# Attention outputs through VectorE's block transposes and transfers instead of TensorE transposes, in an fp32 adaLN transformer block

## The chip, the cores and the metric

The kernel runs on one core of one Trainium2 chip. Its time is the device time of that core in microseconds, as the median of three runs. The core has a matrix engine (TensorE, PE in the profile; its weight loads are listed apart as PEld), a vector engine (VectorE, DVE), a scalar engine (ScalarE, ACT), GpSimd (POOL) and SyncE (SP), which here only issues transfers. All five run their own instruction streams and wait for each other through semaphores. [...]

## What is computed

One block of a transformer with adaptive layer norm, in fp32: 2048 tokens (S), width 576 (D), 32 heads of width 18, a feed-forward width of 4608.

```python
mod = (_silu(c) @ w_mod).reshape(c.shape[0], 6, 1, -1)
h = _layernorm(x, axis=-1) * (1 + ca) + sa
# A: qkv = h @ wqkv, split in heads
scores = jnp.einsum("bhqd,bhkd->bhqk", q, k) * (Dh ** -0.5)
p = _softmax(scores, axis=-1)
o = jnp.einsum("bhqk,bhkd->bhqd", p, v)
x = x + ga * (o @ wo)
h = _layernorm(x, axis=-1) * (1 + cb) + sb
x = x + gb * (_silu(h @ w1) @ w2)
```

The weights are scaled up by factors of 8 and 64, so the scores are large and the maximum of each row of scores must be taken off before the exponential.

## The kernel before

**Arithmetic.** Matrix products run in a fast fp32 format with fewer bits. Each operand is therefore split into a high part, which that format holds exactly, and a low part, and three products are summed (high by high, high by low, low by high).

**Tiling.** The queries are cut in four blocks of 512 (`NQB`), the heads in eight groups of four (`NQUAD`). A *quad* is four heads of one block, so there are 32 quads. Each quad has 32 *slots*, and each slot has two halves, `j` = 0 and 1.

**Two passes over the scores.** A slot of the first pass (`slot_a`, with the matmul on line 678) computes *row scores*: a tile with 128 queries as rows and 512 keys as columns. VectorE takes the maximum over the columns from PSUM (line 680). This pass serves only the maxima. A slot of the second pass (`slot_b`, line 735) computes the scores again with keys as rows and 512 queries as columns, and ScalarE takes the exponential (line 737). The maxima enter the second product as two extra rows of the query tile `qt` (rows 54 and 55 of each half, high and low part), against rows of ones in the key tile `kt`; so the product comes out with the maximum already subtracted. The second pass runs `LEAD` slots behind the first. `LEAD` is 38, so six slots lie between the last maximum of a quad and the first use of the maxima.

**The maxima's way.** After slot 31 of a quad, `max_a` (lines 693 to 700) reduces over the key blocks, negates and splits in two parts. Four half slots later (`MB`), `max_b` transposes them on TensorE into a bank of the row scores' pool (tile `pst`, line 704), VectorE copies them out (`mt`, line 709), and `max_rows` (line 714) places them in `qt` by four transfers.

**The outputs' way.** `pv` (line 772) multiplies the exponentials by V. Each head uses 32 rows of one PSUM bank: 18 output features, one row for the sum of the exponentials, and padding; the 512 queries are the columns. ScalarE copies the bank to `ov` (line 776). Then `out_b` (lines 781 to 801) transposes it on TensorE to queries as rows (`pso`, four transposes into one bank of the row scores' pool), VectorE takes the reciprocals of the sums and multiplies (lines 788 and 794), and the result goes to the block's tile `ot`. `out_b` asks the plan for 440 ns of TensorE; it may be put off by up to 12 half slots. After the eighth quad of a block, `post` queues the block's projection and MLP as *filler*: first `o_T` (lines 859 to 872), which transposes `ot` back to features as rows on TensorE (tile `psT`, 20 transposes a block) and splits it in a high part (ScalarE) and a low part (VectorE); then the projection by `wo` (`proj`, 28 steps for each of four groups of 128 queries), the second layer norm (`ln_a`, `ln_c`), its transposes (`h_T`), and the feed-forward products (`mlp1`, `mlp2`). The last part of a block's second product, 32 items, is held back in a list `left` and put in between the next block's projections: eight ahead of each of the first three, six and two later.

**What sets the order.** TensorE's order is written out: a planner (`Plan`, and the loop at the end of the body) keeps estimates of VectorE's and ScalarE's work and of when PSUM banks come free, and picks among a score step, a PV step and a filler item. The filler is spread over the slots by a pace. The start (`start_tasks`) is ordered by a small list scheduler of its own, and contains the first `LEAD` slots of the first pass. The orders of the other engines and of SP's transfers come from the framework, by priority and by readiness in its own estimate of time. PSUM has two or three banks for row scores, two or three for the second pass, one for PV and one to three for the filler.

**Buffers.** K lies in 14 tiles `kt` (`NKB`), filled eight slots ahead (`KLD`); `qt` has three buffers, `ov` one, and the tile `ot` one. The second layer norm writes its result over `ot`.

Of the kernel before, what the change touches and what calls it, by code (L numbers as in the profile page):

```python
# [39 lines left out]
LEAD = 38  # L40
# [15 lines left out]
MB = 4  # L56
# [3 lines left out]
LP0 = 1000  # L60
LP = 8000
# [271 lines left out]
def tile_adaln_block(ctx: ExitStack, tc: tile.TileContext, x, wqkv, wo, w1, w2, c, wfirst, wcol, out):  # L333
# [348 lines left out]
    def slot_a(s, j):  # L682
        if j == 0:
            slot_load(s)
        t = quads[s // 32]
        slot_mm(s, j)()
        plan.op("V", plan.t + TL - TS, TMAX, plan.take("a"))
        if j == 1 and s % 32 == 31:
            now = 2 * s + 1
            later.append((now, 0, 0, lambda: max_a(t), None))  # L690
            later.append((now + MB, 3, 110, lambda: max_b(t), lambda: t.get("ms_at")))

    def max_a(t):
        negm = at1.tile([P, 4, NST], F32, name="negm", bufs=2)
        nc.vector.tensor_reduce(negm, t["mx"], axis=AX.X, op=ALU.max, negate=True)
        ms = at1.tile([P, 2, 4, NST], F32R, name="ms", bufs=2)
        nc.vector.tensor_copy(ms[:, 0], negm)
        nc.vector.tensor_sub(ms[:, 1], negm, f(ms[:, 0]))
        t["ms"] = ms
        chain([("V", 230), ("V", 180), ("V", 180)], plan.t, None, lambda at: t.update(ms_at=at + TR))  # L700

    def max_t(t):
        ps = aux([P, 512], "pst")
        nc.tensor.transpose(ps[:32, :P], f(t["ms"]).rearrange("p c h s -> p (c h s)"), ident)
        return ps

    def max_copy(t, ps):
        t["mt"] = at1.tile([32, P], F32R, name="mt", bufs=2)
        nc.vector.tensor_copy(t["mt"], ps[:32, :P])

    def max_rows(t):
        for i in range(4):
            r0 = 64 * (i % 2) + 54 + i // 2
            nc.sync.dma_start(f(t["q"][r0:r0 + 1].rearrange("o h (a s) -> o (h a) s", s=P)), f(t["mt"][8 * i:8 * i + 8, :]))

    def max_b(t):
        max_copy(t, max_t(t))
        plan.op("V", plan.t, 270, plan.take("a"))
        max_rows(t)
# [45 lines left out]
    def pv(i, t, k0, n):  # L765
# [8 lines left out]
        if k0 + n == NKT:  # L774
# [4 lines left out]
            later.append((state["now"] + 2, 12, 440, lambda: out_b(i, ov), lambda: t["ov"]))  # L779

    def out_b(i, ov):
        b, qd = divmod(i, NQUAD)
        ps = aux([P, NST, P], "pso")
        for s4 in range(NST):
            nc.tensor.transpose(ps[:, s4, :], ov[:, s4 * P:(s4 + 1) * P], ident)  # L785
        rec = att.tile([P, NST, 4], F32, name="rec", bufs=2)
        psr = ps.rearrange("p s (h c) -> p s h c", h=4)
        nc.vector.reciprocal(rec, psr[:, :, :, DH])
        if qd == 0:
            if b:  # L790
                fill.until("h_T")
            o[b] = att.tile([P, NST, 640], F32, tag="o", name="ot", bufs=1)
        for s4 in range(NST):
            nc.vector.tensor_mul(o[b][:, s4, 72 * qd:72 * qd + 72].rearrange("p (h c) -> p h c", h=4), psr[:, s4, :, :DH],
                                 rec[:, s4, :, None].to_broadcast([P, 4, DH]))
        rel = plan.take("a")
        chain([("V", 260)] + [("V", 225)] * 4, plan.t + 100, None, rel)
        del quads[i]
        if qd == NQUAD - 1:
            nc.gpsimd.tensor_copy(o[b][:, :, D:640], o[b][:, :, 512:D])  # L800
            post(b)
# [48 lines left out]
    def post(b):  # L850
# [4 lines left out]
        ob = o[b]  # L855
# [3 lines left out]
        def o_T(kt):  # L859
# [3 lines left out]
            ps = bank("psT", psF)  # L863
            for j in range(NST):
                nc.tensor.transpose(ps[:, j * P:(j + 1) * P], ob[:, j, kt * P:(kt + 1) * P], ident)
            hi = c["th"][:, kt, :]
            chain([("A", 600), ("V", 690)], plan.t, None, plan.take("f"))
            nc.scalar.activation(hi, ps, AF.Copy)
            if kt < 4:
                nc.vector.tensor_sub(c["tl"][:, kt, :], ps, f(hi))  # L870
            else:
                nc.vector.tensor_sub(hi[64:], ps[64:], f(hi)[64:])
# [30 lines left out]
        def ln_c(j):  # L903
            mv, rs = c["ln", j]
            ln_apply(c["x1"][j], ob[:, j, :], mv[:, 0, :], rs, nc.vector)

        def h_T(kt):
# [5 lines left out]
            for j in range(NST):  # L913
                nc.tensor.transpose(ps[:, j * P:(j + 1) * P], ob[:, j, kt * P:(kt + 1) * P], ident)
# [9 lines left out]
        for kt in range(KT):  # L924
            fl.add(440, lambda kt=kt: o_T(kt), need=bank_need, mode="full")
        if b == 0:
            fl.add(LP0)
        for j in range(NST):
            rest(8 if j < 3 else 0)
            for part in range(len(GP)):  # L930
                fl.add(MMH * len(GP[part]), lambda j=j, part=part: proj(j, part), need={0: pair_need, len(GP) // 2: half_need}.get(part))
# [130 lines left out]
    def start_tasks(st):  # L1062
# [296 lines left out]
        for s in range(LEAD):  # L1359
# [9 lines left out]
            if s == 31:  # L1369
                t0 = add("V", 0.59, lambda: max_a(quads[0]), maxes, 8)  # L1370
                kt_ = tok("a")
                t1 = add("P", 0.11, lambda: d.update(pst=max_t(quads[0])), [t0], 8, take=kt_, mode="full")
                t2 = add("V", 0.27, lambda: max_copy(quads[0], d["pst"]), [t1], 8, free=kt_)
                dma(40e3, lambda: max_rows(quads[0]), [t2], 8)
# [183 lines left out]
```

## Time and profile before

| | |
|---|---|
| median of 3 runs | 2488.08 us (2486.09 to 2492.14) |
| span of the profiled execution | 2488.8 us |
| mean granted TensorE clock in it | 0.992 |
| TensorE busy | 2407.3 us, 97% |
| VectorE busy | 1772.8 us, 71% |
| ScalarE busy | 1501.9 us, 60% |
| GpSimd busy | 611.3 us, 25% |

The profiled execution's own time is given only as its span; it is 0.7 us above the median of the runs. In a row of a group, the text before the first bar is line, engine, operation, output and inputs with shapes, and the count. After the bar come the busy time in us and the mean of one in ns, and after the second bar the idle time of the engine just before these instructions, with what ended it. Timeline rows begin with the start in us and the length in us; "x4" means that four like instructions were merged; brackets give idle time before them. Matmuls overlap, and the profile models their ends. "DMA_DIRECT2D" on SPq is the issuing of a transfer. The first 160 us are the start (layer norm, the first Q, K and V products), then come four attention blocks of about 440 to 540 us, of which the last three have the previous block's MLP beside them; from 2212 us the last block's projection and MLP run alone.

### The profile page before, as it was taken

Reading aid. Unit: us, or ns where it says so; the run is one execution under the profiler, and the core shown is the slowest. Engines: PE = TensorE matmul, PEld = TensorE weight load, DVE = VectorE, ACT = ScalarE, POOL = GpSimd, SP = SyncE. Lnnn points to the kernel's source line nnn. Section 1 sums busy time; section 2 is a strip of 40 time slices with the busy share of each in tenths; the row PEclk is TensorE's granted clock in tenths of the full one; section 3 lists DMA queues with packets and bytes.
Section 4 is the critical chain, followed back from the end, with each engine's and each line's share of the span. In section 5 each row is a group of like instructions: output and inputs, shape, how many; then the busy total and the mean of one; then the engine's idle time right before and its main releaser. Section 6 shows DMA issues by size and latency. Waiting matters only on the chain.

```text
span 2488.8 us, 51319 instructions
## 1 busy us (share of the span) xinstructions
PE 2407.3 (97%) x20192; PEld 1581.2 (64%) x20192; DVE 1772.8 (71%) x3156; ACT 1501.9 (60%) x2736; POOL 611.3 (25%) x753
## 2 busy tenths in 40 slices
PE   6999999998989999999999999999999999999999
PEld 5774444434556666666666666666666666678988
DVE  7878878887777777777877777778777777334333
ACT  4237777776666666666666666666666666742121
POOL 4201011121566566652211111111211111110000
PEclk9999999999899999999999999999999999999999
DMA  7843334342455555553543433432633343226463
GB/s 242 261 135 114 109 110 122 105 150 91 135 182 185 168 180 180 198 168 123 173 145 127 146 124 126 134 132 95 209 127 122 126 162 116 103 101 242 171 221 119
DMA packets 159394, 372.02 MB, mean 149 GB/s; under 512 B 17754, under 2 KB 55034, under 8 KB 159154
## 3 DMA queue, kind: packets, MB, share of 16 engines
q1 hardware_dynamic: 154562, 366.45, 43.8%
q8 instruction: 160, 2.62, 0.4%
q10 hardware_dynamic: 4592, 2.29, 0.3%
q14 instruction: 80, 0.66, 0.1%
HBM read 282.35 MB, written 85.80 MB: 148 GB/s over the span
## 4 chain that ended last, share of the span: by engine, by line
PE 87%; DVE 7%; ACT 2%; issue 1%; POOL 1%; DMA 1%; SPq 0%; ACTq 0%; DVEq 0%; POOLq 0%
PE ps L470 26%; PE psv L772 19%; PE psa L678 14%; PE ps L464 10%; PE psb L735 8%; PE psqk L551 4%; DVE mx L680 3%; PE psv L470 2%; PE psp L470 2%; PE psqk L1211 1%; PE pso L785 1%; PE psv L1211 1%; DVE etmp L987 1%; PE psp L464 1%; ACT pt L737 1%
## 5 line engine op out<-in xcount | busy, mean ns | idle before, releaser
L680 DVE TENSOR_REDUCE mx<-psa 128x1 f32<-128x512 f32 x2048 | 1345.5, 686 | 379.1 <-PE psb L735 278.3
L737 ACT ACTIVATE pt<-psb 128x512 f32<-128x512 f32 x2048 | 1162.2, 598 | 549.5 <-PE psb L735 413.2
L735 PE MATMUL psb<-qt,kt 56*128 56x512 f32 x2048 | 789.8, 429 | 6.7 <-DMA qt<-mt 5.0
L678 PE MATMUL psa<-kt,qt 54*128 54x512 f32 x2048 | 768.0, 425 | 24.7 <-DVE mx L680 20.8
L678 PEld LDWEIGHTS psa<-kt,qt 54*128 54x128 f32 x2048 | 344.1, 185 | 415.2 <-DVE mx L680 275.4
L772 PE MATMUL psv<-pt,vt 128*32 128x512 f32 x4096 | 535.0, 607 | 0.5 <-PE psa L678 0.5
L470 PE MATMUL ps<-w2t,g 64*128 64x288 f32 x4992 | 417.9, 294 | 0.2 <-ACT etmp L980 0.2
L470 PEld LDWEIGHTS ps<-w2t,g 64*128 64x128 f32 x4992 | 387.0, 186 | 36.1 <-issue 12.2
L470 PE MATMUL ps<-hh,w1t 64*128 64x512 f32 x2160 | 385.2, 395 | 0.9 <-POOL hh L405 0.8
L735 PEld LDWEIGHTS psb<-qt,kt 56*128 56x128 f32 x2048 | 348.9, 185 | 39.8 <-ACT pt L737 20.0
L470 PEld LDWEIGHTS ps<-hh,w1t 64*128 64x128 f32 x2160 | 220.7, 186 | 58.2 <-issue 10.6
L990 POOL TENSOR_TENSOR g<-etmp,g 128x512 fp32r<-128x512 f32 x108 | 138.4, 1298 | 405.4 <-ACT g L989 361.7
L895 POOL TENSOR_TENSOR x<-x,gt 128x288 f32<-128x288 f32 x116 | 92.7, 800 | 488.5 <-ACT gt L894 478.5
L772 PEld LDWEIGHTS psv<-pt,vt 128*32 128x32 f32 x4096 | 93.0, 108 | 178.8 <-issue 171.3
L470 PE MATMUL ps<-hl,w1t 64*128 64x512 f32 x864 | 186.5, 394 | 1.0 <-POOL hl L403 1.0
L891 DVE TENSOR_TENSOR x<-ps,x 128x288 f32<-128x288 f32 x184 | 83.9, 456 | 122.3 <-PE ps L464 71.0
L464 PE MATMUL ps<-w2t,g 128*128 128x288 f32 x960 | 130.6, 295 | 1.7 <-ACT g L989 0.9
L464 PEld LDWEIGHTS ps<-w2t,g 128*128 128x128 f32 x960 | 128.6, 188 | 3.3 <-ACT g L989 1.2
L986 ACT ACTIVATE eq<-ps 128x512 f32<-128x512 f32 x36 | 21.6, 599 | 146.3 <-PE ps L464 146.3
L464 PE MATMUL ps<-hh,w1t 128*128 128x512 f32 x360 | 106.9, 390 | 0.5 <-DVE hh L405 0.5
L470 PEld LDWEIGHTS ps<-hl,w1t 64*128 64x128 f32 x864 | 93.5, 186 | 18.0 <-POOL hl L403 2.5
L987 DVE SCALAR_TENSOR_TENSOR etmp<-etmp 128x512 f32<-128x512 f32 x108 | 78.1, 761 | 21.4 <-ACT etmp L986 21.4
(142 smaller groups left out, 2033.4 us busy)
## 6 DMA issues: line engine op xcount, KB each, us to landing
w1t<-w1s SPq DMA_DIRECT2D x108, 640.0 KB
w2t<-w2s SPq DMA_DIRECT2D x108, 576.0 KB
kt<-kscr SPq DMA_DIRECT2D x512, 108.0 KB
w1s<-w1t SPq DMA_DIRECT2D x36, 640.0 KB
w2s<-w2t SPq DMA_DIRECT2D x36, 576.0 KB
vt<-vscr SPq DMA_DIRECT2D x32, 608.0 KB
qt<-qscr SPq DMA_DIRECT2D x128, 108.0 KB
raw<-in_w SPq DMA_DIRECT2D x72, 160.0 KB
```

What stands on the lines that cost most here:

```text
L464: mm(self.ps[late], lhsT=lhsT, rhs=rhs, start=(i == 0), stop=(i == self.n - 1))
L470: done = mm(self.ps[g], lhsT=lhsT[rows], rhs=rhs[rows], start=(s == 0), stop=(s == 2 * self.n - 1))
L551: mm(qk_ps[0], lhsT=w[b][:, kt, :], rhs=(hTl if a else hTh)[:, kt, n * 512:(n + 1) * 512], start=(i == 0), stop=(i == 13))
L678: mm(ps, lhsT=t["q"][64 * j:64 * j + 54, hp, stt * P:(stt + 1) * P], rhs=t["k", kc, hp][64 * j:64 * j + 54, :], start=True, stop=True)
L680: return lambda: nc.vector.tensor_reduce(t["mx"][:, 2 * j + hp, stt, kc:kc + 1], ps, axis=AX.X, op=ALU.max)
L735: mm(ps, lhsT=t["k", kt // 4, hp][64 * e:64 * e + 56, kt % 4 * P:(kt % 4 + 1) * P], rhs=t["q"][64 * e:64 * e + 56, hp, :], start=True, sto ...
L737: nc.scalar.activation(t["P"][kt, hp][:, e, :], ps, AF.Exp, scale=SCALE)
L772: mm(t["ps"][32 * h:32 * h + 32, :], lhsT=t["v"][:, c0:c0 + 32], rhs=t["P"][kt, h // 2][:, h % 2, :], start=(kt == 0), stop=(kt == NKT - 1 ...
L891: nc.vector.tensor_add(c["x1"][j][:, hs], ps, c["x1"][j][:, hs])
L895: nc.gpsimd.tensor_add(c["x1"][j][:, hs], c["x1"][j][:, hs], t)
L987: nc.vector.scalar_tensor_tensor(t, t, 1.0, u, op0=ALU.add, op1=ALU.mult)
L990: (nc.vector if last else nc.gpsimd).tensor_tensor(g[:, 1, :], t, f(g[:, 0, :]), op=ALU.subtract)
```

## The change

- `LEAD` goes from 38 to 40.
- Maxima: `max_a` arranges the two parts so that one VectorE transpose of 32x32 blocks (128x32) gives rows of 32 queries. `max_rows` writes the result to DRAM (`mscr`) in one transfer and reads it back into `qt` by two, in runs of 32 values. The TensorE transpose, its bank, the copy, `max_b` and `MB` go. The transfers are issued right after `max_a`.
- Outputs: `out_b` transposes `ov` by 32x32 blocks on VectorE into a scratch part of the block's tile `ou`. There each head's 32 rows are 32 queries, and the columns are 16 blocks of 32. VectorE takes 16 reciprocals per row; GpSimd multiplies (VectorE for the last quad of a block); VectorE transposes back into `ov`. Transfers from SBUF to SBUF then place each head's 18 rows at the head's features in `ou`, features as rows. A head that crosses a multiple of 128 takes two transfers, and rows of the last, partial group of features are placed twice: 40 transfers a block. `out_b` asks for no TensorE time and runs two half slots after the last PV step.
- `o_T` has no transposes: ScalarE copies the high part from `ou`, and GpSimd subtracts for the low part (in the last block VectorE for even groups). It costs the filler nothing. The first projection of a block waits in the plan for `o["at", b]`, five us after the modelled end of `out_b`'s chain.
- The second layer norm gets a tile of its own (`ob`), which takes turns with `ou` in one buffer.
- The held-back items go 16 ahead of the first projection (`RA`), none between (`RB`), and the rest as before behind the fourth.

```diff
-LEAD = 38
+LEAD = 40
-MB = 4
+RA, RB = 16, 0
...
-            later.append((now, 0, 0, lambda: max_a(t), None))
-            later.append((now + MB, 3, 110, lambda: max_b(t), lambda: t.get("ms_at")))
+            later.append((now, 0, 0, lambda: (max_a(t), max_rows(t)), None))
...
-        nc.vector.tensor_copy(ms[:, 0], negm)
-        nc.vector.tensor_sub(ms[:, 1], negm, f(ms[:, 0]))
+        nc.vector.tensor_copy(ms[:, :, 0], neg)
+        nc.vector.tensor_sub(ms[:, :, 1], neg, f(ms[:, :, 0]))
+        t["mt"] = at1.tile([P, 32], F32, name="mt", bufs=2)
+        nc.vector.transpose(t["mt"], f(ms).rearrange("p j c h -> p (j c h)"))
...
     def max_rows(t):
-        for i in range(4):
-            r0 = 64 * (i % 2) + 54 + i // 2
-            nc.sync.dma_start(f(t["q"][r0:r0 + 1].rearrange("o h (a s) -> o (h a) s", s=P)), f(t["mt"][8 * i:8 * i + 8, :]))
+        scr = dram.tile([P, 32], F32, name="mscr", bufs=2)
+        nc.sync.dma_start(scr, t["mt"])
+        for j in range(2):
+            src = scr.rearrange("(g j r) t -> j r g t", g=4, j=2)[j]
+            dst = t["q"][64 * j + 54:64 * j + 56].rearrange("c h (a g t) -> c (h a) g t", g=4, t=32)
+            nc.sync.dma_start(f(dst), src)
...
-            later.append((state["now"] + 2, 12, 440, lambda: out_b(i, ov), lambda: t["ov"]))
+            later.append((state["now"] + 2, 0, 0, lambda: out_b(i, ov), None))
...
-        ps = aux([P, NST, P], "pso")
-        for s4 in range(NST):
-            nc.tensor.transpose(ps[:, s4, :], ov[:, s4 * P:(s4 + 1) * P], ident)
...
+        tt = ou[:, 4, :]
+        nc.vector.transpose(tt, ov)
+        blocks = tt.rearrange("p (b c) -> p b c", c=32)
+        rec = att.tile([P, 16], F32, name="rec", bufs=2)
+        nc.vector.reciprocal(rec, blocks[:, :, DH])
+        eng = nc.vector if qd == NQUAD - 1 else nc.gpsimd
+        eng.tensor_tensor(blocks[:, :, :DH], blocks[:, :, :DH], rec[:, :, None].to_broadcast([P, 16, DH]), op=ALU.mult)
+        nc.vector.transpose(ov, tt)
...
+                for r in (r0, r0 + 64) if kt == 4 else (r0,):
+                    nc.sync.dma_start(ou[r:r + n, kt, :], ov[p0:p0 + n, :])
...
-            ps = bank("psT", psF)
-            for j in range(NST):
-                nc.tensor.transpose(ps[:, j * P:(j + 1) * P], ob[:, j, kt * P:(kt + 1) * P], ident)
-            hi = c["th"][:, kt, :]
-            nc.scalar.activation(hi, ps, AF.Copy)
+            hi, src = c["th"][:, kt, :], o[b][:, kt, :]
+            nc.scalar.activation(hi, src, AF.Copy)
+            eng = nc.vector if last and kt % 2 == 0 else nc.gpsimd
             if kt < 4:
-                nc.vector.tensor_sub(c["tl"][:, kt, :], ps, f(hi))
+                eng.tensor_tensor(c["tl"][:, kt, :], src, f(hi), op=ALU.subtract)
...
-            fl.add(440, lambda kt=kt: o_T(kt), need=bank_need, mode="full")
+            fl.add(0, lambda kt=kt: o_T(kt))
+        rest(RA)
...
-            rest(8 if j < 3 else 0)
+            rest(RB if j else 0)
...
-                t1 = add("P", 0.11, lambda: d.update(pst=max_t(quads[0])), [t0], 8, take=kt_, mode="full")
-                t2 = add("V", 0.27, lambda: max_copy(quads[0], d["pst"]), [t1], 8, free=kt_)
-                dma(40e3, lambda: max_rows(quads[0]), [t2], 8)
+                dma(80e3, lambda: max_rows(quads[0]), [t0], 8)
```

56 lines of the change are left out of this document (24 added, 32 removed).

## The prediction

> **What bounds the kernel now.** I read the page's busy times first, then the chain of work that ended last, then busy times by stretch.
>
> ```profile
> span 2488.8 us, 51319 instructions
> PE 2407.3 (97%) x20192; PEld 1581.2 (64%) x20192; DVE 1772.8 (71%) x3156; ACT 1501.9 (60%) x2736; POOL 611.3 (25%) x753
> PE 87%; DVE 7%; ACT 2%; issue 1%; POOL 1%; DMA 1%; SPq 0%; ACTq 0%; DVEq 0%; POOLq 0%
> ```
>
> ```profile
> 170.00:600.00 430.00, 416.46 (x2482) 171.88 (x2475) 344.13 (x601) 311.65 (x594) 60.45 (x61) 0.99 0.36 118
> 670.00:1140.00 470.00, 459.75 (x4308) 304.16 (x4305) 358.18 (x593) 315.43 (x571) 286.54 (x397) 1.00 0.54 178
> 1225.00:1680.00 455.00, 452.74 (x4303) 303.12 (x4297) 346.63 (x583) 312.48 (x566) 68.68 (x66) 1.00 0.40 135
> ```
>
> The rows give PE, PEld, DVE, ACT and POOL busy time per stretch, then granted clock and DMA share. TensorE is the bound: 99.5% busy in the third row (the third quarter of the attention, with the second block's MLP beside it), 97% in the first, and 87% of the chain is its own work. So PE time that is taken away shortens the run one for one, unless what replaces it makes PE wait. VectorE is second, 80% busy in the first row.
>
> **What leaves PE.** Three kinds of transposes go: the attention outputs (`pso`, 4 a quad, 32 quads), the maxima (`pst`, 1 a quad), and the normalised outputs before the projection (`psT` at line 865, 20 a block, 4 blocks). PE instructions overlap, so I price a piece by the distance from its start to the start of the next work. The first two rows below are a `pso` and its successor, the next two a `pst`, the rest the `psT` of the first block.
>
> ```profile
> 219.91 0.66 PE L785 MATMUL pso<-ident,ov 128*128 128x128 f32 x4
> 220.50 1.07 PE L772 MATMUL psv<-pt,vt 128*32 128x512 f32 x8
> 1401.74 0.28 PE L704 MATMUL pst<-ident,ms 128*32 128x128 f32 x1
> 1401.96 0.73 PE L470 MATMUL ps<-hh,w1t 64*128 64x512 f32 x4
> 598.86 1.47 PE L865 MATMUL psT<-ident,ot 128*128 128x128 f32 x12
> 600.26 0.49 PE L678 MATMUL psa<-kt,qt 54*128 54x512 f32 x1
> 600.92 0.66 PE L865 MATMUL psT<-ident,ot 128*128 128x128 f32 x4 [0.17 <-DVE tl L870]
> 601.51 0.50 PE L678 MATMUL psa<-kt,qt 54*128 54x512 f32 x1
> 602.23 0.63 PE L865 MATMUL psT<-ident,ot 128*128 128x128 f32 x4 [0.22 <-DVE tl L870]
> 602.79 1.07 PE L772 MATMUL psv<-pt,vt 128*32 128x512 f32 x8
> ```
>
> 32 x 0.59 = 18.9 us; 32 x 0.22 = 7.0 us; 4 x (1.40 + 0.59 + 0.56) = 10.2 us. Sum 36.1 us.
>
> **Waits that go with them.** The groups by line and shape show how long PE (and the weight load, PEld) sat idle just before them, for a PSUM bank that VectorE had not yet read:
>
> ```profile
> L785 PE MATMUL pso<-ident,ov 128*128 128x128 f32 x128 | 21.0, 286 | 3.2 <-DVE mx L680 3.2
> L785 PEld LDWEIGHTS pso<-ident,ov 128*128 128x128 f32 x128 | 13.4, 140 | 13.5 <-DVE mx L680 10.0 <-issue 3.1 <-ACT pt L737 0.4
> L704 PE MATMUL pst<-ident,ms 128*32 128x128 f32 x32 | 9.1, 284 | 3.4 <-DVE mx L680 2.8
> L865 PE MATMUL psT<-ident,ot 128*128 128x128 f32 x80 | 11.1, 278 | 2.3 <-DVE tl L870 2.1
> ```
>
> PE's own idle time is 3.2 + 3.4 + 2.3 = 8.9 us. The next row score uses the same bank, so some of the wait only moves to it: I take 5 us. The ends are 0 and 15 us (the 8.9, plus half of PEld's 13.5, which is partly covered by the matmul still streaming).
>
> **What VectorE gets.** These are its rows for what leaves and for the nearest of what comes:
>
> ```profile
> L788 DVE RECIPROCAL rec<-pso 128x16 f32<-128x16 f32 x32 | 8.1, 253 | 13.2 <-PE pso L785 12.7
> L794 DVE TENSOR_TENSOR ot<-pso,rec 128x72 f32<-128x72 f32 x128 | 21.0, 224 | 1.3
> L709 DVE CAST mt<-pst 32x128 fp32r<-32x128 f32 x32 | 8.6, 269 | 0.0
> L870 DVE TENSOR_TENSOR tl<-psT,th 128x512 fp32r<-128x512 f32 x16 | 10.4, 681 | 1.4 <-ACT th L868 1.4
> L990 DVE TENSOR_TENSOR g<-eq,g 128x512 fp32r<-128x512 f32 x36 | 24.9, 692 | 20.1 <-ACT g L989 19.9
> L990 POOL TENSOR_TENSOR g<-etmp,g 128x512 fp32r<-128x512 f32 x108 | 138.4, 1298 | 405.4 <-ACT g L989 361.7 <-PE psb L735 31.3 <-PE psa L678 11.7
> L392 DVE TENSOR_SCALAR ot<-x,mv,rs 128x576 f32<-128x576 f32 x16 | 9.2, 577 | 0.4
> ```
>
> Per quad 0.253 + 4 x 0.224 + 0.269 = 1.42 us leave. Two block transposes of 128x512 come; no row shows one. Between 0.52 (0.577 x 512/576, a one-input pass) and 1.38 (twice 0.69) I take the two-input pass of the same size, 0.69. With the reciprocal 0.25 and a 128x32 transpose at 0.25 (the 32x128 cast's 0.27 is nearest) that is 1.88 us, 0.46 more a quad, 14.7 us in all. Of the 20 subtractions at lines 870 and 872, 17 go to POOL: 17 x 0.68 = 11.6 us less. Four multiplications (the last quad of a block) come, estimated at 288/512 x 0.69 = 0.39 each. Net some 5 us more on VectorE. [...] With a quarter of VectorE idle in two of the three stretches I charge 1 us; the ends are -3 (0.52 each) and 11 us (1.38 each is 44 us more, a quarter of it felt by PE, an assumption).
>
> The second transpose must wait for a POOL multiplication, about 0.80 us as the 128x288 row says, and behind it on VectorE stand the row-score reductions that free PE's banks. Instructions are issued as they become ready, not as written: a reduction stands between the parts of one max step here.
>
> ```profile
> 1397.21 0.17 DVE L697 CAST ms<-negm 128x16 fp32r<-128x16 f32 x1
> 1397.29 0.68 DVE L680 TENSOR_REDUCE mx<-psa 128x1 f32<-128x512 f32 x1
> 1397.89 0.16 DVE L698 TENSOR_TENSOR ms<-negm,ms 128x16 fp32r<-128x16 f32 x1
> L895 POOL TENSOR_TENSOR x<-x,gt 128x288 f32<-128x288 f32 x116 | 92.7, 800 | 488.5 <-ACT gt L894 478.5
> ```
>
> So other reductions can stand between the two transposes. 28 quads x 0.1 = 3 us; ends 0 and 28 x 0.80 = 22 us.
>
> **The maxima's rows by DRAM.** Now VectorE, four transfers, landing; then VectorE, one write to DRAM, two reads of it. In the tightest quad of the first block the stages before were:
>
> ```profile
> 361.14 0.22 DVE L695 TENSOR_REDUCE negm<-mx 128x16 f32<-128x64 f32 x1
> 366.56 3.42 SPq L714 DMA_DIRECT2D qt<-mt  x4
> 371.26 0.47 PE L735 MATMUL psb<-qt,kt 56*128 56x512 f32 x1 [0.67 <-DMA qt<-mt]
> 27.58 0.81 SPq L1347 DMA_DIRECT2D oscr<-full  x1
> 31.56 2.20 SPq L1349 DMA_DIRECT2D kt<-oscr  x7
> ```
>
> The last issue ended at 369.98, 1.3 us before PE ran. A write to DRAM was followed by a read that needs it within 31.56 - 27.58 = 4.0 us. New chain: 1.1 for four small VectorE steps + 4.0 + two issues at 0.8 + 1.3 = 8.0 us (the 1.1 is 0.22 + 0.17 + 0.16 + 0.25 and gaps); runs of 128 bytes may add up to 3. There were 371.26 - 361.14 = 10.1 us for the six slots from the last maximum to the first use (38 - 32); eight slots at the same 1.7 us are 13.5 us. It fits by 2 to 5 us, so I charge 0; the ends are -0.7 (the wait in that row goes) and 16 us (eight quads of the first block 2 us late). SP issues three instead of four for this, and some 160 placements more in all, five a quad at about 0.3 us (2.20/7); what stands behind a waiting one are loads of K, Q, V and weights; K's have eight slots of lead. I put nothing on the queue itself: each placement takes its turn after `ov` is ready, and only a block's last is soon read.
>
> **Block joins, tail, start.** The `out_b` step no longer waits for a PE slot, so a block's end comes some us sooner; but the projection now waits for placements to land, ACT copies and five POOL subtractions of 1.3 us (against 0.68 on VectorE). At three of the four block ends 16 held-back second-layer items run first and cover most of this; the first has none. In the tail the last `ov` and the projection stand 11 us apart already:
>
> ```profile
> 2211.99 0.60 ACT L776 ACTIVATE ov<-psv 128x512 f32<-128x512 f32 x1 [4.46 <-PE psv L772]
> 2223.60 0.43 PE L464 MATMUL psp<-wo,th 128*128 128x288 f32 x2
> ```
>
> I charge 3 us; ends -6 and 20. Two more slots before the main loop move four reductions (2.7 us) to the start: 1 us, ends 0 and 2.7. LEAD 40 makes K's 14 buffers free just as the load is due: a group of K is used for the last time in the slot before, and the load still has eight slots (13.5 us as above) to land: nothing. The separate tile for the second layer norm takes the outputs' place only after the copies of `o_T`, which already stood ahead of it: nothing, as is the new order of the held-back items inside a block, where PE has the same work.
>
> **Sum.** 36 + 5 - 1 - 3 - 0 - 3 - 1 = 33 us off the profiled 2488.8, so 2455.8; the median of the runs is 0.7 us below that span, so 2455 us.
>
> **Rivals.**
> *VectorE is held by POOL* (the other side). POOL runs in its order too, and stands long for others:
>
> ```profile
> POOL g L990 <- ACT g L989: 361.7, 32, 16.7
> ```
>
> That is us in total, times, the longest. If the multiplication stands behind such an instruction, the second transpose holds VectorE, and after two or three banks PE stands. The forecast's gain is gone at 33/28 = 1.2 us of PE per quad, and 1.5 us make it slower by over 0.3%. At 2 us: 2455 - 3 + 56 = 2508. For it: POOL is 61% busy in the second stretch. Against it: POOL is 14 to 15% busy in the others, and issue follows readiness. Chance 0.13.
>
> *Maxima come late.* Three dependent transfers stand in one SP queue with weight loads. Each us late costs 8 us in the first block, 32 in all: 3 us late in the first block gives 2479. Against it stands the 2 to 5 us of room. Chance 0.10.
>
> [...] The same subtraction took VectorE 692 ns above, and this long where POOL did its share of it:
>
> ```profile
> L403 DVE TENSOR_TENSOR hTl<-etmp,hTh 128x512 fp32r<-128x512 f32 x8 | 9.4, 1174 | 0.3
> ```
>
> So POOL work can lengthen VectorE's. 28 x 0.80 + 17 x 1.3 = 44.5 us come to POOL; if VectorE lost them all and PE felt a half, 22 us, the time is 2477. [...] Chance 0.06.
>
> *Nothing comes of it*: the freed PE time turns into waits for exponentials and reductions, 2488. The first row with 80% VectorE speaks for it, the 99.5% against. Chance 0.07.
>
> **How the numbers follow.** Forecast 0.60 (2436 to 2472); faster still, as the waits go whole, 0.04; late maxima 0.10 and port 0.06, both still faster; nothing 0.07; held 0.13. Faster than 0.3% (7.5 us, about what a measurement here can tell): 0.80; same 0.07; slower 0.13. The range 2434 to 2484 leaves out the held case, nothing, and little else.
>
> **What would show it.** Right: PE's busy time down by about 36 us, no `pso`, `pst` or line-865 rows, `DMA` waits of `psb` under 5 us, block transposes near 0.69 us, and small idle of them on POOL. Wrong: VectorE idle for POOL in the tens of us, `psa` weight loads waiting more than before, `psb` waiting for `qt`, or PE idle between a block's last `ov` and its projection by over 5 us a block.

## The result and the profile after

The changed kernel takes 2576.7 us (median, 2575.4 to 2578.2) against 2487.1 us for the kernel before: 3.59% slower (ratio 1.0359, 95% interval 1.0345 to 1.0374). The forecast was 2455 us, 2434 to 2484. It is wrong in sign, by 122 us.

The page of the changed kernel, cut to the span, the busy times and the granted clock in 40 slices of the span:

```profile
span 2575.4 us, 51091 instructions
PE 2409.2 (94%) x19952; PEld 1576.6 (61%) x19952; DVE 1785.8 (69%) x3079; ACT 1499.4 (58%) x2736; POOL 648.6 (25%) x794
PEclk9999999988899999998899999999999999998999
```

and the clock row of the kernel before:

```profile
PEclk9999999999899999999999999999999999999999
```

TensorE executes 240 matmuls fewer and yet is busy as long as before (2409 against 2407 us): part of its work ran at half clock (mean granted clock 0.970, where the kernel before had 0.992). The 8s stand at the first, the second and the last join of the blocks (slices of 64 us from 515, 1159 and 2318 us). The joins, and the stretch where the first MLP's weights are converted (second row), in busy time per engine (PE, PEld, DVE, ACT, POOL, then clock, DMA share, GB/s), first after, then before. The fifth row is the tail's join; the sixth is a steady stretch.

```profile
590.00:680.00 90.00, 68.30 (x532) 40.10 (x532) 57.57 (x114) 42.80 (x76) 31.15 (x45) 0.85 0.26 85
810.00:1000.00 190.00, 172.18 (x1572) 113.09 (x1574) 131.63 (x211) 115.69 (x210) 106.62 (x149) 0.96 0.50 166
1165.00:1275.00 110.00, 85.24 (x777) 57.17 (x771) 67.98 (x131) 52.75 (x95) 25.23 (x28) 0.86 0.39 123
1725.00:1830.00 105.00, 84.44 (x792) 56.93 (x790) 68.97 (x133) 53.78 (x97) 25.21 (x28) 0.89 0.40 130
2285.00:2345.00 60.00, 41.17 (x254) 37.86 (x247) 28.97 (x70) 10.29 (x17) 11.09 (x14) 0.80 0.42 152
1320.00:1700.00 380.00, 375.86 (x3548) 248.05 (x3546) 292.72 (x478) 258.04 (x472) 60.97 (x61) 1.00 0.41 139
```

```profile
590.00:680.00 90.00, 82.33 (x653) 47.24 (x651) 72.75 (x145) 55.96 (x98) 31.51 (x46) 0.92 0.29 96
810.00:1000.00 190.00, 188.30 (x1771) 124.20 (x1767) 146.16 (x241) 130.32 (x237) 119.11 (x165) 1.00 0.54 178
1160.00:1270.00 110.00, 106.80 (x1032) 70.78 (x1030) 88.26 (x170) 71.54 (x129) 24.10 (x28) 1.00 0.44 143
1700.00:1805.00 105.00, 101.94 (x989) 68.30 (x987) 84.57 (x164) 68.89 (x125) 24.09 (x27) 1.00 0.45 150
2215.00:2275.00 60.00, 55.52 (x352) 49.53 (x349) 35.45 (x84) 15.62 (x26) 9.13 (x13) 1.00 0.57 204
1300.00:1680.00 380.00, 377.84 (x3610) 254.00 (x3608) 288.77 (x487) 260.17 (x472) 57.85 (x56) 1.00 0.39 133
```

The steady row is as full as before. In the 110 us of the second join TensorE does 777 matmuls where it did 1032. Nearly all of the loss is at the joins and in the first MLP's conversion: outside them, and after the start, gaps longer than 0.7 us come to 6.6 us in the changed kernel.

**A ledger.** I add up two things over each trace: the gaps (idle of TensorE longer than 0.7 us between two of its instructions) and half the time that the clock record shows at half clock outside those gaps.

| kernel | span us | gaps us | half clock us | sum us |
|---|---|---|---|---|
| before | 2488.8 | 20.0 | 21.2 | 41.2 |
| after | 2575.4 | 119.0 | 52.6 | 171.6 |
| difference | +86.6 | +99.0 | +31.4 | +130.4 |

The sum grew by 130.4 us and the span by 86.6, so 43.8 us of work are gone. That is about the gain that was forecast; waits and half clock took it back three times over. The gaps over 0.8 us of the changed kernel, put together by what ended the wait, are these five (101 us of 117; 8 of the other 16 are in the start, as before; the cause of the third row is read from the trace, and no run isolates it):

| wait | where | us |
|---|---|---|
| a load of `x` whose place in SBUF was not yet free | second, third and fourth join | 33.4 |
| VectorE, held by a multiply on POOL | 826 to 1040, and once in each later block | 20.2 |
| row scores behind other work on VectorE, mostly the second layer norm's steps | joins | 20.0 |
| `g` of the last hidden matmul | start of the three later joins | 15.8 |
| placements of the last quad, and copies that wait for them | first join | 11.9 |

The waits of the changed kernel that carry these (total us, times, longest), the last one SP's:

```profile
PEld psa L678 <- DVE mx L680: 332.3, 400, 11.0
PE psa L678 <- DVE mx L680: 66.3, 47, 10.7
DVE ov L786 <- POOL ou L785: 39.5, 20, 7.7
DVE x L886 <- DMA x<-in_x: 28.5, 3, 9.8
ACT th L862 <- DMA ou<-ov: 26.5, 7, 5.8
SPq L709 <- DMA mscr<-mt: 65.7, 32, 8.1
```

and the first two in the kernel before:

```profile
PEld psa L678 <- DVE mx L680: 275.4, 370, 1.7
PE psa L678 <- DVE mx L680: 20.8, 41, 0.9
```

The longest wait of a row score for its reduction was 0.9 us; it is 10.7 us now.

### The profile page after: what moved, and what is told of

Same layout as the page of the kernel before. It is cut to its first block, busy times and chain, and to the rows that moved or that the text cites. A ratio compares the mean times of both kernels' runs of the same rounds, so it can differ in the third digit from the quotient of the medians.

```text
span 2575.4 us, 51091 instructions
## 1 busy us (share of the span) xinstructions
PE 2409.2 (94%) x19952; PEld 1576.6 (61%) x19952; DVE 1785.8 (69%) x3079; ACT 1499.4 (58%) x2736; POOL 648.6 (25%) x794
## 5 line engine op out<-in xcount | busy, mean ns | idle before, releaser
L678 PE MATMUL psa<-kt,qt 54*128 54x512 f32 x2048 | 779.1, 430 | 71.5 <-DVE mx L680 66.3
L725 PE MATMUL psb<-qt,kt 56*128 56x512 f32 x2048 | 799.5, 434 | 5.7 <-ACT pt L727 4.1
L762 PE MATMUL psv<-pt,vt 128*32 128x512 f32 x4096 | 544.9, 613 | 0.0
L470 PE MATMUL ps<-w2t,g 64*128 64x288 f32 x4992 | 427.5, 297 | 24.9 <-DVE x L886 11.5
L470 PEld LDWEIGHTS ps<-w2t,g 64*128 64x128 f32 x4992 | 397.1, 189 | 64.4 <-DVE x L886 13.2
```

Of the source, the lines that this page charges most:

```text
L470: done = mm(self.ps[g], lhsT=lhsT[rows], rhs=rhs[rows], start=(s == 0), stop=(s == 2 * self.n - 1))
L678: mm(ps, lhsT=t["q"][64 * j:64 * j + 54, hp, stt * P:(stt + 1) * P], rhs=t["k", kc, hp][64 * j:64 * j + 54, :], start=True, stop=True)
L725: mm(ps, lhsT=t["k", kt // 4, hp][64 * e:64 * e + 56, kt % 4 * P:(kt % 4 + 1) * P], rhs=t["q"][64 * e:64 * e + 56, hp, :], start=True, sto ...
L762: mm(t["ps"][32 * h:32 * h + 32, :], lhsT=t["v"][:, c0:c0 + 32], rhs=t["P"][kt, h // 2][:, h % 2, :], start=(kt == 0), stop=(kt == NKT - 1 ...
```

## The experiments

**The buffer wait at the joins.** The second join of the changed kernel on SP, VectorE and TensorE (start, duration, the instruction, and in brackets the idle time ahead of it):

```profile
1235.22 0.32 SPq L705 DMA_DIRECT2D mscr<-mt  x1
1245.23 1.38 SPq L709 DMA_DIRECT2D qt<-mscr  x2
1246.71 0.37 SPq L1011 DMA_DIRECT2D out<-x  x1
1248.90 0.34 SPq L846 DMA_DIRECT2D x<-in_x  x1
```

```profile
1251.87 0.46 DVE L886 TENSOR_TENSOR x<-psp,x 128x288 f32<-128x288 f32 x1 [9.78 <-DMA x<-in_x]
```

```profile
1254.19 0.79 PE L678 MATMUL psa<-kt,qt 54*128 54x512 f32 x1 [10.74 <-DVE mx L680]
```

The fourth projection adds into `x1[3]`. `x1` has five places, so this one waits until the old `x1[2]` has had its last product added and is stored. That product is the 24th of the 32 held-back items. It stood ahead of the third projection; now, with 16 items first and none between the projections, it stands behind the fourth. VectorE waits 9.8 us for the load, the reductions wait behind the add, and TensorE waits for a bank. SP makes it longer: it stood from 1235.5 to 1245.2 us, until the maxima's write had landed, with the store of `x` behind it (the first 1.9 us are put down to a weight load). One kernel restores the order, one gives `x1[3]` of the second and fourth block a place of its own:

```diff
-        rest(RA)
...
-            rest(RB if j else 0)
+            rest(8 if j < 3 else 0)
```

> The changed kernel with the held-back items back in the old order (eight ahead of each of the first three projections, none ahead of all). Theory A, the fourth projection waits for its x tile, whose buffer comes free only when the third held-back group is done: the three stalls of 10.7, 8.7 and 14.0 us before row scores and psT go, and with them some 20 us of half clock behind them; 2576 - 33 - 20 = about 2523 us, and the mean clock rises from 0.970 to about 0.977. Rival, VectorE held by POOL carries the loss: the three stalls shrink but time stays above 2560.

Measured: 2540.8 us (ratio 1.0217, 1.0169 to 1.0266), clock 0.978.

```diff
-            c["x1"].append(pool.tile([P, D], F32, name="x1", bufs=5))
+            c["x1"].append(ga if b % 2 and j == 3 else pool.tile([P, D], F32, name="x1", bufs=5))
```

> The changed kernel, its order of items kept, with a sixth place for the x tiles (the tile of the first gate, idle by then, holds the fourth x tile of the second and fourth blocks). Theory A: the wait of VectorE for x (28.5 us) goes, as with the old order, about 2523 us. Rival, it is the order and not the buffer (projections back to back crowd VectorE): the stalls stay and the time is above 2560; between the two, both have a part.

Measured: 2541.2 us (1.0219, 1.0170 to 1.0268), clock 0.978. Both take some 36 us off the changed kernel, and in both VectorE's wait for the load of `x` is gone from the list of waits. Order and place are two ends of one cause. The gain is less than the 53 us expected: gaps fell by some 30 us and half clock by 11 to 13.

**VectorE held by POOL.** The first of the three long holds, on VectorE and on POOL:

```profile
819.64 1.22 DVE L680 TENSOR_REDUCE mx<-psa 128x1 f32<-128x512 f32 x2
826.19 0.71 DVE L786 STREAM_TRANSPOSE ov<-ou 128x512 f32<-128x512 f32 x1 [5.34 <-POOL ou L785]
```

```profile
821.65 1.57 POOL L828 TENSOR_TENSOR raw<-raw,gb 128x288 f32<-128x288 f32 x2 [0.83 <-DMA raw<-in_w]
823.17 0.87 POOL L830 TENSOR_TENSOR w1t<-raw,w1t 128x320 fp32r<-128x320 f32 x1
823.99 0.79 POOL L829 CAST w2t<-raw 128x288 fp32r<-128x288 f32 x2
824.74 0.79 POOL L830 TENSOR_TENSOR w2t<-raw,w2t 128x288 fp32r<-128x288 f32 x1
825.49 0.67 POOL L785 TENSOR_TENSOR ou<-ou,rec 128x288 f32<-128x288 f32 x1
```

The multiply takes 0.67 us, but it stands behind weight conversions, one of which waits for its weights to land. VectorE stands for 5.3 us at the second transpose with the reductions behind it. The edit puts all 32 multiplies on VectorE:

```diff
-        eng = nc.vector if qd == NQUAD - 1 else nc.gpsimd
+        eng = nc.vector
```

> The changed kernel with the multiplication of the outputs on VectorE in all quads, so that VectorE waits for POOL no more between its transposes. Theory B, VectorE is held by POOL: the 39.5 us of VectorE idle before the second transpose go, with PE stalls of 3.1, 5.9, 7.1 and 1.4 us three times (20 us) and 8 us of half clock; about 2548 us. Rival: the 28 multiplications of 0.46 to 0.77 us (13 to 22 us on VectorE) cost as much as they save, 2565 to 2580.

Measured: 2554.7 us (1.0274, 1.0225 to 1.0322), clock 0.976: 22 us faster than the changed kernel, with the wait `DVE ov <- POOL ou` gone. The two edits together:

> The sixth place for x1 and the multiply on VectorE together. Theory (the buffer wait and the queue on POOL are two causes that share no time): the gains of the two single edits add, 2576.7 - 35.5 - 22.0 = 2519, mean clock about 0.984. Rival (they share the half-clock time, or one only makes room for the other): 2535 or above.

Measured: 2517.2 us (1.0124, 1.0107 to 1.0141), clock 0.983; 2519 was expected. The gains of the two edits add.

**The parts apart.** The maxima's part alone, in the kernel before, with the row scores 40 slots ahead:

```diff
-LEAD = 38
+LEAD = 40
...
-            later.append((now, 0, 0, lambda: max_a(t), None))
-            later.append((now + MB, 3, 110, lambda: max_b(t), lambda: t.get("ms_at")))
+            later.append((now, 0, 0, lambda: (max_a(t), max_rows(t)), None))
```

> The kernel before with the maxima's part of the change alone (VectorE transpose, DRAM and back, LEAD 40). Forecast's step: 32 x 0.22 us of PE and some waits go, about 2477 us. Rival, the trip through DRAM holds SP and what stands behind it: 2487 us or more, and psb or x waits for transfers.

Measured: 2472.6 us (0.9939, 0.9918 to 0.9960), clock 0.995. It is faster than both kernels. Part of its gain is a wait of the kernel before that the prediction did not count, for the maxima's four transfers:

```profile
PE psb L735 <- DMA qt<-mt: 5.0, 2, 4.3
```

The long one stood at 725 us and had 3.41 us of half clock behind it, from 730.2 us; with the maxima's part neither is there. And the outputs' part alone, which is the changed kernel with these lines, and the functions behind them, turned back:

> The changed kernel with the maxima's part as it was (transposed on TensorE, copied, four transfers) and the row scores 38 slots ahead: the outputs' part alone. Theory (the two parts add): the maxima's part alone gave 15 us, so 2576.7 + 15 = 2592. Rival (the maxima's trip through DRAM holds SP at the joins and so costs there, with the new outputs): 2577 or below.

Measured: 2556.5 us (1.0279, 1.0256 to 1.0301), clock 0.972. The parts do not add: the outputs' part costs 69 us alone, the maxima's part gains 15 alone, and together they cost 90, which is 35 more than the sum. (The outputs' part alone also has the row scores 38 slots ahead again; no run separates the lead from the way of the maxima.) The trace shows part of how. Without the trip through DRAM the same store and load at the second join were issued at:

```profile
1241.31 0.34 SPq L1022 DMA_DIRECT2D out<-x  x1
1244.42 0.33 SPq L857 DMA_DIRECT2D x<-in_x  x1
1247.96 2.05 SPq L715 DMA_DIRECT2D qt<-mt  x3
```

ahead of the maxima's transfers (the view ends before the fourth of them), not behind them. The gap there was 4.2 us instead of 10.7, at the third join 5.5 instead of 8.7. These 9.8 us are over half of the 17.8 us of gaps by which the two traces differ; the rest is spread. That the trip through DRAM costs anything where `x1` has its own place was not tried.

**Waits for `g` and for the placements.** Two rows of the changed kernel, at the second and the first join:

```profile
1175.08 0.85 PE L470 MATMUL ps<-w2t,g 64*128 64x288 f32 x4 [4.24 <-ACT g L992]
```

```profile
594.77 0.85 PE L470 MATMUL psp<-wo,th 64*128 64x288 f32 x4 [5.89 <-ACT th L862]
```

The held-back products read the `g` of the hidden matmul that ran just ahead; the transposes of `o_T` used to stand between (with the old order back, this wait was still 4.2 us, so it is not the order). The first projection reads `th`, whose last columns come by placements. To the run with two edits I added two due times for the planner:

```diff
+            c["g_at"] = plan.t + 7000
...
-... at + 5000}))
+... at + (14000 if b == 0 else 5000)}))
```

> The run with the two edits, and besides the planner told when two inputs are ready: the first held-back product not before its g (7.0 us behind the last hidden matmul), the first projection of block 0 not before its placements have landed (14.0 us behind the last quad's chain instead of 5.0). Theory (the waits of 4.2, 4.2 and 2.9 us for g and of 5.0 + 3.9 us for th at the first join are idle TensorE that row scores could fill, and each drags half-clock windows behind it): some 20 us of gaps and some 12 us of clock go, 2519 - 32 = 2487, clock about 0.990. Rival (the planner moves the waits elsewhere): 2510 or above.

Measured: 2515.0 us (1.0110, 1.0088 to 1.0131), clock 0.978: no gain that can be told. The waits for `g` at the second and third join fell from 6.4 and 5.4 us to 2.7 and 3.2, but shorter ones (1.1 to 2 us) stood in their place and half clock grew from 34 to 48 us. The wait for `th` did not move (4.9 + 4.1 us): the time that the first projection's need reads is set by a callback that has not yet run for the last quad, so it holds the value of the quad before, which is long past. The need in the changed kernel thus held nothing back. Set for the last quad alone, with the last two copies into `th` held by it too:

```diff
+        o["at", b] = None
-... lambda at: o.update({("at", b): at + 5000}))
+... lambda at: o.update({("at", b): at + 8000}) if last_q else None)
...
+        for kt in range(3, KT):
+            fl.add(20, lambda kt=kt: o_T(kt), need=lambda: o["at", b])
```

> The changed kernel with the last two copies into th and the first projection held back until the last quad's placements have landed, and nothing else. Theory (the waits of 5.9 and 3.1 us at the first join come from that alone): 9 us of gaps and some 5 us of clock go, 2576.7 - 14 = 2563. Rival (the held-back items at the later joins move with it, and the buffer wait grows): 2577 or above.

Measured: 2572.9 us (1.0338, 1.0315 to 1.0360), clock 0.971. The two gaps of 5.9 and 3.1 us are gone, but a gap of 3.2 us for the exponentials came, and waits elsewhere grew by part of it (for the load of `x` 28.5 to 31.2 us on VectorE). Of the 14 us expected, 4 came, and the two intervals overlap.

**What an idle TensorE costs.** In the kernel before, I held a row score with a chain of small memsets on POOL, begun when the matmul ahead had ended:

```diff
+        if j == 0 and 230 <= s < 806 and s % 36 == 14:
+            for n in range(60):
+                hold = nc.gpsimd.memset(idle, 0.0)
+                if n == 0:
+                    tc.add_manual_dep(hold.ins, state["mm"].ins.name, SYNC, reason="the slot before")
...
+            tc.add_manual_dep(state["mm"].ins, hold.ins.name, SYNC, reason="a hold")
```

> The kernel before, with 16 holds: every 36 slots from slot 230 on, a row-score matmul waits for a chain of 60 small memsets on POOL that starts when the matmul ahead of it has ended (estimate 4 to 6 us each, to be read from the trace as the gap on TensorE). Theory (an idle TensorE of that length is followed by windows of half clock, so that a gap costs more than itself): the time grows by the gaps' sum and by another 1.7 to 5 us for each, 27 to 80 us in all, and the mean clock falls from 0.992 to 0.96 to 0.98. Rival (the half clock does not come from the gaps): it grows by no more than the gaps' sum, and the clock stays at 0.99.

Measured: 2729.3 us (1.0977, 1.0951 to 1.1002), clock 0.954. The holds came out longer than meant: a memset took 104 ns on the mean, but they began 161 ns apart in ten of the 16 chains and up to 330 ns in the others, and some chains stood behind other POOL work. The 16 came to 200.6 us. The time grew by 242 us, so by 2.6 us for each gap beyond the gap itself. One of them, as a row of TensorE and as windows (busy times and clock):

```profile
1837.31 0.79 PE L684 MATMUL psa<-kt,qt 54*128 54x512 f32 x1 [8.96 <-POOL idle L681]
```

```profile
1828.30:1832.20 3.90, 0.05 (x2) 0.00 (x0) 0.34 (x1) 0.17 (x1) 2.52 (x25) 1.00 0.00 0
1832.20:1837.20 5.00, 0.00 (x0) 0.00 (x0) 0.00 (x0) 0.00 (x0) 3.21 (x32) 0.50 0.00 0
1837.30:1842.40 5.10, 5.09 (x27) 2.64 (x29) 1.99 (x4) 1.61 (x3) 0.79 (x1) 0.50 0.02 4
1842.40:1870.00 27.60, 27.60 (x268) 18.43 (x268) 20.49 (x36) 17.78 (x33) 1.59 (x2) 1.00 0.51 168
```

The clock halves 3.9 us into the gap and stays so for 5.1 us of work after it: 27 matmuls, where the next 27.6 us hold 268. The same in 64 shorter pieces, every 9 slots and of 15 memsets:

> The kernel before, with 64 holds of 15 memsets each, every 9 slots over the same stretch: the same idle time in pieces of a quarter. Theory (only a gap that fills about a window of 3.4 us is answered by the half clock): the time grows by the gaps' sum alone, within 10 us, clock 0.985 or above, so less than with the 16 long holds. Rival (the idle share counts, not the length of a gap): the clock falls as with the long holds.

Measured: 2872.2 us (1.1551, 1.1520 to 1.1582), clock 0.936. The idle time was not the same as in the long holds: the 64 came to 274.6 us, 4.3 us on the mean: many of 2 to 2.5 us, and some of 5 to 20 behind POOL work. The time grew by 385 us, 110 more than the gaps, 1.7 us for each. My theory that short gaps go free does not hold. Counted over this trace after 200 us (a gap has half clock with it when such a window covers its end or begins within 4 us of it):

| gap | gaps | with half clock |
|---|---|---|
| 0.7 to 1.2 us | 11 | 0 |
| 1.2 to 1.7 us | 10 | 3 |
| 1.7 to 2.2 us | 16 | 12 |
| 2.2 to 3 us | 15 | 12 |
| over 3 us | 24 | 24 |

**All of it mended.** With the multiply on VectorE, the old spread of the held-back items, and both due times right:

```diff
+        rest(8)
+        for kt in range(3, KT):
+            fl.add(20, lambda kt=kt: o_T(kt), need=lambda: o["at", b])
...
+            rest(8 if 0 < j < 3 else 0)
```

> The outputs' part with every wait found so far taken out: the multiply on VectorE, held-back items 8 ahead of each of the first three projections, the first held-back product not before its g, and the last two copies into th and the first projection not before the placements of the last quad have landed (the time for it is now the last quad's; in the changed kernel and in the run before it was read one quad too early, so that it held nothing back). Theory (the work saved on TensorE is there, about 37 us against the kernel before, and waits and half clock took it back): of the 68 us of gaps and 34 us of clock in the run with two edits about 25 and 15 go, 2517 - 40 = 2477, so below the kernel before. Rival (new waits take their place): 2500 or above.

Measured: 2509.1 us (1.0081, 1.0065 to 1.0097), clock 0.983: 8 us better than with two edits, where 40 were expected. New waits of 1 to 3 us came at the joins (row scores behind the second layer norm's VectorE chain), so the rival was nearer. Three more edits: a dependency that keeps the copies into `th` behind the last quad's own copy on ScalarE, all held-back items first in the last block, and a slower pace at the first join:

```diff
-            fl.add(LP0)
-        rest(8)
+            fl.add(4000)
+        rest(24 if last else 8)
...
+            tc.add_manual_dep(done.ins, state["ov"].ins.name, SYNC, reason="not ahead of the last quad")
```

> The run with every wait taken out, and three things more: the first three copies into th not ahead of the last quad's own copy on ScalarE (one had held ScalarE and the exponentials at 541 us), in the last block all 24 held-back items ahead of the last copies (a wait of 4.5 us for th), and the first join's items spread (4000 instead of 1000 in the pace). Theory (the outputs' part can be made free of its waits, and only their price stands between it and the 37 us of saved TensorE work): 8 us of gaps and about 10 us of clock go, 2509 - 18 = 2491. Rival (what is left is the price of a join without TensorE work of its own, wherever the items stand): 2503 or above.

Measured: 2490.6 us (1.0007, 0.9997 to 1.0017), clock 0.986: as fast as the kernel before. The 2491 expected was met in part by luck: of its 8 us of gaps and 10 of half clock, 2.4 and 10.7 came (the ledger below), and a new wait of 8.0 us for `g` stood in the tail. The page's busy times of this kernel, and of the one with the maxima's part alone:

```profile
PE 2383.9 (96%) x19952; PEld 1559.1 (63%) x19952; DVE 1796.0 (72%) x3107; ACT 1497.9 (60%) x2736; POOL 631.8 (25%) x766
```

```profile
PE 2394.0 (97%) x20160; PEld 1578.0 (64%) x20160; DVE 1773.1 (72%) x3156; ACT 1496.9 (61%) x2736; POOL 612.6 (25%) x753
```

The ledger over all runs; "work" is the change of the span less the change of the sum, both against the kernel before:

| kernel | span us | gaps | half clock | sum | work |
|---|---|---|---|---|---|
| after | 2575.4 | 119.0 | 52.6 | 171.6 | -43.8 |
| old order | 2539.4 | 87.9 | 40.1 | 128.0 | -36.2 |
| a place for `x1` | 2538.2 | 89.3 | 41.3 | 130.6 | -40.0 |
| multiply on VectorE | 2552.7 | 103.3 | 40.2 | 143.5 | -38.4 |
| the last two | 2513.2 | 68.3 | 34.1 | 102.4 | -36.8 |
| and due times | 2514.2 | 58.7 | 48.0 | 106.7 | -40.1 |
| need alone | 2574.2 | 112.8 | 53.4 | 166.2 | -39.6 |
| outputs' part alone | 2563.8 | 101.2 | 53.3 | 154.5 | -38.3 |
| maxima's part alone | 2470.9 | 24.1 | 11.7 | 35.8 | -12.5 |
| mended | 2502.6 | 52.2 | 39.0 | 91.2 | -36.2 |
| spread | 2484.1 | 49.8 | 28.3 | 78.1 | -41.6 |
| long holds | 2727.1 | 223.4 | 53.1 | 276.5 | +2.9 |
| short holds | 2873.7 | 296.2 | 128.6 | 424.8 | +1.4 |

The two kernels with holds, which save no work, close to within 3 us, so the sum accounts for the time. Every kernel with the new outputs has 36 to 44 us of work less. What differs among them is in the main waits and half clock. Each row is one trace: that of the outputs' part alone ran 9 us above the median of its runs, those of "mended" and "spread" 5 us below. The two parts' work, 38.3 and 12.5, adds to 7 us more than the 43.8 of both together, so a row of work is known to some 7 us.

## Why the prediction was wrong

**What leaves PE, the waits with it, and VectorE's net price: right in sum.** These were 36 + 5 - 1 = 40 us; the ledger has 36 to 44. The groups by line and shape of the changed kernel show the prices that I had bounded:

```profile
L786 DVE STREAM_TRANSPOSE ov<-ou 128x512 f32<-128x512 f32 x32 | 22.7, 709 | 39.8 <-POOL ou L785 39.5
L780 DVE STREAM_TRANSPOSE ou<-ov 128x512 f32<-128x512 f32 x32 | 22.5, 702 | 8.9 <-ACT ov L766 8.9
L785 POOL TENSOR_TENSOR ou<-ou,rec 128x288 f32<-128x288 f32 x28 | 18.9, 675 | 129.3 <-DVE rec L783 111.0 <-PE psb L725 8.5 <-DMA qt<-qscr 7.5
L700 DVE STREAM_TRANSPOSE mt<-ms 128x32 f32<-128x32 f32 x32 | 6.7, 209 | 0.8
L725 PE MATMUL psb<-qt,kt 56*128 56x512 f32 x2048 | 799.5, 434 | 5.7 <-ACT pt L727 4.1
```

A block transpose of 128x512 took 0.70 to 0.71 us (0.69 was taken). VectorE's busy time rose by 13 us, not 5, so that term was too small. No run shows the "port" to which the prediction gives 0.06. The trace of the kernel before shows a lengthening: of the ten subtractions of line 403 on VectorE, the five that began beside an idle POOL took 0.69 us each, and the five that began while POOL ran the same subtraction 1.64 to 1.68 us. In the changed kernel the reductions of line 680 took 691 ns at the median, as before (690), and the 13 us are far from the 44.5 that VectorE was to lose.

**The maxima by DRAM: right on the path, wrong on the queue.** `psb` has no wait for `qt` among its releasers above; the up to 3 us for runs of 128 bytes were my estimate, and no run isolates them. Alone this part gained 15 us, where its run's expectation was 10; the wait of 4.3 us at 725 us and the half clock behind it are some 6 of them. But "I put nothing on the queue itself" failed. SP stood 65.7 us in 32 waits for the write to land, up to 8.1 us at once, and with the new outputs it stood in front of the store and load that a join needed. Turning the maxima's part back gave 20 us. In the kernel before with the maxima's part alone SP stood 70.0 us in the same 32 waits and the time fell, so the stand cost only where something urgent was behind it. The 160 placements were priced low too: 0.72 us of SP each at the median, not 0.3, and SP stood 41.3 us in nine waits for `ov`; what that cost, no run shows.

**"28 quads x 0.1 = 3 us" for VectorE behind POOL: mis-sized by seven times.** The argument was that other reductions stand between the two transposes. Two stand in the row ahead of the hold shown, and then VectorE stood 5.3 us all the same. VectorE idled 39.5 us in 20 waits, and taking POOL out gave 22 us. This was the rival on the other side, with its mechanism as described. It named POOL's wait for ScalarE's `g`; six holds of 1.8 to 1.9 us stood behind two subtractions for `g`, and the three longest, 19.6 us together, stood in the second stretch, where POOL also converts weights. The rival was held to decide the sign alone, and it does not: without it the kernel is still 2.7% slower.

**"I charge 3 us" for the joins, and "nothing, as is the new order of the held-back items": the steps that failed.** The order cost 36 us, by two runs that undo it from either end. I asked whether TensorE has the same work, not which tile each item frees. The transposes that left had also been cover. At the second join of the kernel before, 10.1 us with 20 of them lay between the last hidden matmul and the first held-back product (1142.55 to 1152.64 us), and `g` was finished in that time; in the changed kernel it is 1.6 us with none (1168.27 to 1169.87), and TensorE waits for `g` 4.2 us. That the copies into `th` were covered likewise is argued from the order. I counted the transposes as cost alone. And the need that was to hold the first projection read a time that was already past.

**No term for the clock.** Half clock grew by 31 us in the changed kernel, and the sum has nothing for it. The holds show that it follows the gaps: 1.7 to 2.6 us for each beyond the gap. In the long hold shown, half clock began 3.9 us after the gap did; in the short holds, 24 of the 31 gaps of 1.7 to 3 us had half clock with them. The clock records show more. In each of the 14 traces (before, after and the twelve runs) the stretches of half clock, 259 in all, begin on one grid of 3.413 us, and those that end within the trace last one to eight of its steps. With one such step as a window, here is what the window behind got, by TensorE's idle time in a window (5972 of some 9700 windows of the 14 traces after 200 us; the ends of matmuls are modelled, so the middle rows are rough):

| idle in a window | next at half, if this one is full | next at half, if this one is half |
|---|---|---|
| under 0.4 us | 0 of 4737 | 44 of 168 |
| 0.4 to 0.8 us | 1 of 430 | 26 of 29 |
| 0.8 to 1.2 us | 5 of 139 | 17 of 17 |
| 1.2 to 1.8 us | 45 of 120 | 32 of 32 |
| over 1.8 us | 151 of 151 | 149 of 149 |

In the traces of before and after alone, with every window counted, the middle column is 0 of 1204, 1 of 66, 1 of 20, 4 of 10 and 14 of 14. Half clock followed every full window with over 1.8 us of idle time, about half a window, in one gap or in several: twelve full windows came to over 1.8 us of idle by pieces that were all under 1.5, and half clock followed all twelve. One gap that the grid cuts in two went free: the 2.0 us at 677 us of the short holds, cut into 1.4 and 0.6, had none. Behind a window at half, 0.4 to 0.8 us of idle was mostly followed by half again (26 of 29). A window at half clock takes 1.7 us of work, half of 3.41, as much as the short holds cost beyond themselves on the mean.

**What stays open.** With the waits that were found taken out, the kernel with both parts comes to a span of 2484.1 us, 13 us above the maxima's part alone (18 by the medians of the runs), with 29 us of work less. The ledger puts 26 us of gaps and 17 of half clock between the two. Whether an order exists in which the joins without their transposes stand free of waits was not found.

## What to carry to other kernels

Before work is taken from the engine that bounds, list what was finished while it ran, and what else stands on each queue that takes the work over: here the transposes cost 2.5 us a block and stood, with the work between them, over 10 us in which `g` was finished. An item that moves carries its buffer's release with it, so a new order is priced by the loads that wait for the buffers, not by the work in it. Price a wait of the bounding TensorE of 2 us and more at the wait plus some 2 us of half clock (1.7 to 2.6 in the holds), since over 1.8 us of idle in one window of 3.41 us was followed by half clock in 151 of 151 full windows here, and try the parts of a change one by one: here one part was worth 15 us alone and the other hid it.

## What was not expected of the hardware

- Half clock came with gaps of 1.7 to 2.2 us already, in 12 of 16 cases, and not below 1.2 us (0 of 11). 64 holds of 4.3 us on the mean cost 1.7 us each beyond themselves, 16 of 12.5 us cost 2.6.
- A write to DRAM followed by its read in one queue took 10.0 us at the second join (issue at 1235.22, next issue at 1245.23), behind weight loads issued up to 1233.91, where 4.0 us had been read at the kernel's start (27.58 to 31.56 in the kernel before).
- The stretches of half clock began on one grid of 3.413 us in each of the 14 traces. Of its windows, 151 of 151 full windows with over 1.8 us of idle TensorE were followed by half clock, and 1 of 5167 with under 0.8 us.
- A memset of 128x8 on POOL took 104 ns on the mean, and a chain of them one every 161 ns where nothing else stood between.
